# One attention block and two gated products on one core: the first pair's output product in seven products, and some steps put first in program order

## The chip, the cores and the metric

The kernel runs on one core of one Trainium2 chip. The metric is device time in microseconds, from the start to the end of one execution; lower is better. The engines are named as the profile names them: PE (TensorE's matmuls), PEld (its weight loads), DVE (VectorE), ACT (ScalarE), POOL (GpSimd) and SP (SyncE, which issues nearly all transfers). PSUM has eight banks here of 128 x 512 numbers: b0 to b3 and acc0 to acc3.

## The reference

Everything is float32. Attention is of the linear kind: 8 batches, 8 heads, 576 positions, 64 features.

```
q_s = softmax of q over the features;  k_s = softmax of k over the positions
kv  = k_s^T v          (64 x 64 for each head)
x   = q_s kv           -> 4608 rows of 512
layer one:  y = (silu(x w_gate) * (x w_val)) w_out                  (512 -> 1536 -> 512)
layer two:  out = max(max(y w1, y w2), y w3) w_out2                 (512 -> 768 -> 512)
```

## The kernel before, in words

**Tiling.** The 4608 rows are nine blocks of 512. `BLOCKS` puts them in six stages: blocks 0, 1 and 2 alone, then the pairs 3+4, 5+6 and 7+8 (stages 3, 4 and 5; the first, second and third pair). In a stage the weights' columns are taken 128 at a time, F1 = 12 such tiles in layer one and F2 = 6 in layer two; p counts them by twos. A float32 product is made of three matmuls: each operand is split into a high part (a copy rounded by ACT, "hi") and a low part (the rest, a subtraction, "lo"), and high x high, high x low and low x high are summed in PSUM.

**Seven products for eight.** In a pair, the gate, value and layer-two products of a 2 x 2 arrangement of blocks are computed in seven products by Strassen's method in Winograd's form (`wino_unit`, line 1529, and `product`, line 707): sums of row blocks (t1 to t4) times sums of weight blocks, and the results put together by copies and additions that read the PSUM banks (`wino_copy`, `wino_add`, lines 806 to 818). The weights' sums are made once: stage 3 makes their parts as it goes (`make_job`, line 1458; the instructions stand at lines 681 and 685) and stores them, stages 4 and 5 load them (`wino_load_job`).

**The output product of layer one** ("O") multiplies the hidden tiles h = silu(gate) * value by w_out. Stage 3 does it in eight products: `outs` (line 1636) runs `out_product` (line 721, the matmuls at line 736) for each of 12 hidden tiles, 4 column groups and 2 halves, 3 matmuls each; the hidden tiles are split by `hidden_job` (line 1482; instructions at 789 and 803). The stages in `OUT_WINO = (4, 5)` do it in seven: `factors` (line 1676) runs `factor_product` (line 741, the matmuls at line 748) for 6 pairs of tiles, 7 products, 2 column groups, 3 matmuls each. Its left sums of hidden tiles are made by `eager` and `second_job` (lines 1361 and 1395; the instruction is `minus`, line 757), its splits by `factor_hidden_job` (line 1342; instructions at 796 and 799), and its results are put together by `out_wino` (line 1736). The sums of w_out that it needs are made in stages 1 and 2 (`SUMS_AT`) and stored. Stage 3 in the old form ends the output with `y_wino_0`, `y_wino_1` and `y_wino_late` (lines 1915 to 1951), which make layer two's operands b11 to t4.

**What sets the order of the work.** The kernel is written out by a planner that runs when the kernel is built. `walk` (line 983) goes through the list of matmul groups in PE's order, with an estimate of the time of each. Jobs that feed a group (loads, splits, differences) stand in queues (`ahead`) and are taken some microseconds before their use. Each job books time on an engine in the plan:

```
do(e, t, dur, fn)      line 881: looks for a gap of length dur at or after t, and puts the instruction there
soon(e, t, dur, fn)    line 891: books the same gap, but puts the instruction into program order at t
best(t, cost, fn)      line 901: do, on the engine (DVE or POOL, or ACT) that would end first
```

So `do` leaves what was booked earlier in front, and `soon` passes it. The engines then run their instructions in the order written, each waiting for its own semaphores; the planned times themselves are not on the chip. `soon` reports `min(u, begin) + dur`: the end as if the step began at t, or where the operation that runs at t ends.

**What empties a bank.** `wino_unit.end` (in line 1529 on) and `consumed` (line 1503) book the copy, addition, product or maximum that reads a finished bank; a later product of the same bank waits for it.

**Attention** for the next stage runs as three chains of steps (`k_steps` and `q_steps`, lines 1092 and 1132) beside the present one: maximum, subtraction, exponential, sum, multiplication, transposition, split. `advance` (line 1032) books the steps of a chain that are due up to `LOOK` (2.0 us in stage 0, 1.4 later) ahead; `slot` (line 1020) puts a chain's matmuls (`kv_mm`, line 270; `x_mm`, lines 433 to 435) into PE's order where a bank is offered. Stage 5 has none of it.

**Memory.** Tiles are claimed by tag; a claim waits for the last reader of the tile that had the place. Tags that matter here: "or" (four places of 128 x 512, weights and sums on their way), "hh" (three places for a split hidden tile), "xr" (the rows of a pair, and later sums), "s00" to "s11" (four tiles of gate values).

## Time and profile before

| what | us |
|---|---|
| median of three runs | 1521.42 |
| lowest and highest run | 1520.96 and 1523.5 |
| the profiled execution | 1522.33 |
| its span, first to last instruction | 1520.5 |
| PE busy in the span | 1458.5 (96%) |
| DVE busy | 1097.2 (72%) |
| ACT busy | 697.2 (46%) |
| mean granted clock of PE | 0.992 |

The profile is of one execution. Rows of "busy time by stretch" give the stretch in microseconds from the span's start, its length, then for each engine its busy time and, in brackets, the number of instructions; then PE's granted clock, the DMA engines' share and GB/s. Where such a row is of one line alone, only the engines that the line uses stand there. Rows of "groups of instructions" give line, engine, operation, the tile written and the tiles read, the shapes and the count, then busy time and mean duration in ns, then the engine's idle time just before them and what ended it. Matmuls are pipelined: 390 ns is the length of one from its own start to its end, and the next begins before that.

### The profile page before, as it was taken

The page shows a single profiled execution, that of the slowest core. Times are in us where ns is not written, and L with a number is a line of the kernel's source. Part 1 is how long each engine was busy: PE and PEld are TensorE (multiplying, and loading weights), DVE is VectorE, ACT ScalarE, POOL GpSimd, SP SyncE. Part 2 cuts the span into 40 slices and gives each one's busy share as a digit, 9 for nine tenths or more (in the row PEclk, how much of TensorE's full clock was granted, in tenths as well). Part 3 has the DMA queues.
Part 4 walks back from the last instruction along what each step waited for, and adds up shares of the span by engine and source line. Part 5 has one row for each costly group of instructions (what it writes and reads, how often), then busy time and mean ns, then how long its engine had stood idle before and what let it go on. Part 6 is the DMA issues. An engine that isn't in the chain of part 4 may idle for free.

```text
span 1520.5 us, 20625 instructions
## 1 busy us (share of the span) xinstructions
PE 1458.5 (96%) x6834; PEld 1177.2 (77%) x6834; DVE 1097.2 (72%) x1879; ACT 697.2 (46%) x1196; POOL 80.4 (5%) x70
## 2 busy tenths in 40 slices
PE   2899999999999999999999989999999999999998
PEld 1666688888878888878877867888877778888887
DVE  7869996787777678676579885677887755578553
ACT  3758774554566535535443344334532332245112
POOL 1000000000000000000012040000000300000000
PEclk9899999999999999999999999999999999999999
DMA  7798878878788899988578777775776576657764
GB/s 193 201 274 298 275 235 231 257 238 256 217 283 269 289 372 307 280 268 238 180 215 259 222 221 202 209 207 160 222 207 173 177 223 195 191 160 220 208 202 148
DMA packets 318729, 349.01 MB, mean 230 GB/s; under 512 B 158368, under 2 KB 197280, under 8 KB 318624
## 3 DMA queue, kind: packets, MB, share of 16 engines
q1 hardware_dynamic: 313824, 346.52, 75.2%
q10 hardware_dynamic: 4800, 1.18, 0.4%
q8 instruction: 55, 0.90, 0.3%
q14 instruction: 50, 0.41, 0.1%
HBM read 257.16 MB, written 90.44 MB: 229 GB/s over the span
## 4 chain that ended last, share of the span: by engine, by line
PE 78%; DVE 8%; DMA 6%; ACT 5%; issue 2%; SPq 1%; ACTq 0%; DVEq 0%
PE pb L715 52%; PE pacc L736 11%; PE pacc L748 4%; PE pb L736 4%; PE pb L748 3%; DMA stage<-in_moe_w_out_dram 1%; PE pkv L270 1%; PE pacc L728 1%; ACT plain L528 1%; DMA plain<-raw_V 1%; DVE hlo L803 1%; DVE tall L818 1%; DMA v_sb<-in_v_dram 1%; DMA stage<-in_moe_w_gate_dram 1%; ACT L774 1%
## 5 line engine op out<-in xcount | busy, mean ns | idle before, releaser
L715 PE MATMUL pb<-b11h,wall 128*128 128x512 f32 x756 | 270.1, 398 | 13.1 <-ACT wall L565 6.4
L818 DVE TENSOR_TENSOR tall<-tall,pb 128x512 f32<-128x512 f32 x234 | 159.9, 684 | 158.6 <-PE pb L715 146.7
L715 PE MATMUL pb<-b21h,wall 128*128 128x512 f32 x756 | 265.1, 393 | 0.0
L715 PEld LDWEIGHTS pb<-b11h,wall 128*128 128x128 f32 x756 | 142.7, 189 | 50.6 <-ACT wall L565 8.4
L715 PEld LDWEIGHTS pb<-b21h,wall 128*128 128x128 f32 x756 | 143.1, 189 | 30.7 <-ACT tall L808 0.4
L808 ACT COPY tall<-pb 128x512 f32<-128x512 f32 x117 | 68.8, 588 | 196.8 <-PE pb L715 158.6
L715 PE MATMUL pb<-b11l,wall 128*128 128x512 f32 x378 | 148.6, 393 | 0.0
L715 PE MATMUL pb<-b21l,wall 128*128 128x512 f32 x378 | 148.0, 391 | 0.0
L568 DVE TENSOR_TENSOR wall<-plain,wall 128x512 fp32r<-128x512 f32 x126 | 86.5, 689 | 38.1 <-ACT wall L565 37.5
L565 ACT CAST wall<-plain 128x512 fp32r<-128x512 f32 x126 | 77.1, 618 | 63.8 <-DVE plain L547 22.8
L736 PE MATMUL pacc<-hhi,ow 128*128 128x512 f32 x304 | 98.9, 389 | 0.1
L715 PE MATMUL pb<-t3h,wall 128*128 128x512 f32 x252 | 88.5, 392 | 3.0 <-DVE tall L818 2.9
L789 ACT CAST hhi<-tall 128x512 fp32r<-128x512 f32 x74 | 45.5, 618 | 98.3 <-DVE tall L783 79.1
L736 PE MATMUL pacc<-ow,hhi 128*128 128x512 f32 x288 | 89.0, 390 | 0.0
L715 PE MATMUL pb<-t1h,wall 128*128 128x512 f32 x252 | 88.8, 393 | 0.0
L715 PE MATMUL pb<-b22h,wall 128*128 128x512 f32 x252 | 88.7, 392 | 0.0
L715 PE MATMUL pb<-t2h,wall 128*128 128x512 f32 x252 | 88.5, 392 | 0.0
L715 PE MATMUL pb<-t4h,wall 128*128 128x512 f32 x252 | 88.0, 390 | 0.0
L715 PEld LDWEIGHTS pb<-b11l,wall 128*128 128x128 f32 x378 | 71.4, 189 | 15.2 <-issue 1.2
L715 PEld LDWEIGHTS pb<-b21l,wall 128*128 128x128 f32 x378 | 71.5, 189 | 14.5
L783 DVE TENSOR_TENSOR tall<-s,pb 128x512 f32<-128x512 f32 x81 | 54.9, 679 | 19.4 <-PE pb L715 15.1
L803 DVE TENSOR_TENSOR hlo<-tall,hhi 128x512 fp32r<-128x512 f32 x69 | 49.5, 718 | 26.4 <-ACT hhi L789 25.8
(279 smaller groups left out, 3001.5 us busy)
## 6 DMA issues: line engine op xcount, KB each, us to landing
wall<-wino_W SPq DMA_DIRECT2D x153, 256.0 KB, 3.1
wall<-wino_G SPq DMA_DIRECT2D x102, 256.0 KB, 3.2
wall<-wino_V SPq DMA_DIRECT2D x102, 256.0 KB, 3.0
ow<-parts_O SPq DMA_DIRECT2D x33, 512.0 KB, 5.5
ow<-parts_P SPq DMA_DIRECT2D x32, 512.0 KB, 5.1
wino_W<-wall SPq DMA_DIRECT2D x63, 256.0 KB, 4.5
ow<-owino SPq DMA_DIRECT2D x48, 256.0 KB, 3.5
wino_G<-wall SPq DMA_DIRECT2D x42, 256.0 KB, 4.4
```

The lines of the kernel that those rows point to most:

```text
L270: nc.tensor.matmul(out=c["pkv"][u * D:(u + 1) * D, g, :], lhsT=lhsT, rhs=rhs, start=i == 0, stop=i == R,)
L528: nc.scalar.activation(out=plain[conv[i]], in_=high.bitcast(F32), func=AF.Abs, scale=2.0 ** -112)
L565: nc.scalar.copy(out=wall[:, i:i + 2, 0], in_=plain[kind, f].rearrange("p (a n) -> p a n", a=2))
L568: eng.tensor_tensor(out=wall[:, i:i + 2, 1], in0=plain[kind, f].rearrange("p (a n) -> p a n", a=2), in1=wall[:, i:i + 2, 0], op=ALU.subtract,)
L715: nc.tensor.matmul(out=banks[bank], lhsT=a, rhs=b, start=start and n == 0, stop=stop and n == 5, skip_group_check=True,)
L736: nc.tensor.matmul(out=banks[bank], lhsT=lhsT, rhs=rhs, start=first and n == 0, stop=last and n == 2)
L748: nc.tensor.matmul(out=banks[bank[e]], lhsT=w[:, a, es], rhs=h[b], start=first and n == 0, stop=last and n == 2, skip_group_check=True,)
L783: eng.tensor_tensor(out=hidden_tile(kind, f, half, tmp), in0=s, in1=a(), op=ALU.mult if kind == "V" else ALU.max)
L789: nc.scalar.copy(out=hid[key][0], in_=st["h", key[1], key[2], key[3]])
L803: eng.tensor_tensor(out=lo, in0=st.pop(("h", key[1], key[2], key[3])), in1=hi, op=ALU.subtract)
L808: nc.scalar.copy(out=tall[:, i], in_=banks[bank])
L818: eng.tensor_tensor(out=out_, in0=tall[:, x], in1=banks[bank] if isinstance(bank, str) else tall[:, bank], op=ALU.add)
```

## The change

The list of stages that do layer one's output product in seven products, `OUT_WINO`, gets stage 3. There the tiles for the differences of p = 2 to 5 are claimed under s00 to s11 once the last value product has read them (`have["s read"]`), not under "or", which stage 3 needs for weights; two splits late in the product go to "hh" instead of "or"; the order of the differences is 5, 4, 2, 3; and the new rows' tile is claimed only when the plan's last reader of the old one has ended (`have["x end"]`). Splits of hidden tiles are kept in the order of their claims (`have["hid order"]`). Operations that empty a PSUM bank on DVE (`consumed`, `wino_unit.end`) are booked by `soon` instead of `do`, and so are the steps of attention's chains in stages 0 to 4 (`HURRY`), on DVE and ACT. Steps that go by `best` are not touched. Products 6 and 5 of a unit are kept in the plan behind two additions (`T["c22"]`, `T["c12"]`).

```diff
@@ -842,7 +842,7 @@
     ENG = {"D": nc.vector, "G": nc.gpsimd, "A": None}
     DVE_LATE = 1.0
     HASTE = 5.0
-    EASY = ()
+    HURRY = (0, 1, 2, 3, 4)
     SWITCH = 8.0
     X_WAIT = 0.0
     OWN = 1.0
@@ -1065,9 +1065,9 @@
                 ch["t"] = best(ch["t"], {"D": dur, "G": 2.0 * dur}, fn)
             elif e in ("D+", "D="):
                 t, ch["i"] = take(ch["t"])
-                ch["t"] = do("D", t, dur, fn, ch["i"])
+                ch["t"] = (soon if len(marks) - 1 in HURRY else do)("D", t, dur, fn, ch["i"])
             else:
-                ch["t"] = do(e[0], ch["t"], dur, fn)
+                ch["t"] = (soon if len(marks) - 1 in HURRY else do)(e[0], ch["t"], dur, fn)
             if e in ("D-", "D="):
                 drop(ch["i"], ch["t"])
             if DEBUG:
@@ -1343,7 +1343,7 @@
         if key not in ready or not (home or left("hh")):
             return False
         t, a, then = ready[key]
-        t = max(t, use - 9.0)
+        t = max(t, use - 9.0, 0.0 if home else have.get("hid order", 0.0))
         if home == ("or", "or"):
             if not left("or", 2):
                 return False
@@ -1353,6 +1353,8 @@
         if not home:
             t, have["hh", key] = acquire("hh", t)
         t = do("A", t, 0.62, factor_hi, key, a, home)
+        if not home:
+            have["hid order"] = t - 0.62 - LAT + 0.01
         there["hid", key] = t = do("D", t, 0.69, factor_lo, key, a)
         if then:
             then(t)
@@ -1393,7 +1395,8 @@
             have.pop(("t1 of", p))()
 
     def second_job(use, s, p):
-        if ("B", p, 0, 1) not in have or not (p < 2 or left("or")):
+        tight = s == 3
+        if ("B", p, 0, 1) not in have or not (p < 2 or tight or left("or")):
             return False
         if ("t1 of", p) in have:
             have.pop(("t1 of", p))()
@@ -1401,6 +1404,10 @@
         t = max(ready[s, "O", p, 1][0], use - 9.0)
         if p < 2:
             a2, then = lambda: xr_slot(6 + p), None
+        elif tight:
+            t = max(t, have["s read"])
+            at(t - 0.01, spare_slot, p, ("s00", "s01", "s10", "s11")[p - 2])
+            a2, then = lambda: more[p], None
         else:
             t, o = acquire("or", t)
             at(t - 0.01, spare_slot, p)
@@ -1419,19 +1426,14 @@
 
     more = {}
 
-    def spare_slot(p):
-        more[p] = sb.tile([128, TB], F32, tag="or", name="t2f", bufs=4)
+    def spare_slot(p, tag="or"):
+        more[p] = sb.tile([128, TB], F32, tag=tag, name="t2f", bufs=4 if tag == "or" else 1)
 
...
@@ -1482,12 +1484,14 @@
     def hidden_job(use, key):
         if key not in ready or not left("hh"):
             return False
-        t, h = acquire("hh", max(ready[key], use - 9.0))
-        if use - t < HASTE and key[1:] not in EASY:
+        t, h = acquire("hh", max(ready[key], use - 9.0, have.get("hid order", 0.0)))
+        if use - t < HASTE:
+            have["hid order"] = t + 0.01
             t = soon("A", t, 0.62, hidden_hi, key)
             there["hid", key] = t = soon("D", t, 0.69, hidden_lo, key, nc.vector)
         else:
             t = do("A", t, 0.62, hidden_hi, key)
+            have["hid order"] = t - 0.62 - LAT + 0.01
             there["hid", key] = t = best(t, COST, hidden_lo, key, by=use - 1.5)
         if ("tmp", key) in have:
             drop(have.pop(("tmp", key)), t)
@@ -1517,7 +1521,8 @@
         if kind == "V" and not psum:
             t = best(t, COST, consume, kind, p, i, half, a, tmp)
         else:
-            t = do("D", t, 0.69, consume, kind, p, i, half, a, tmp, nc.vector)
+            t = soon("D", t, 0.69, consume, kind, p, i, half, a, tmp, nc.vector)
+        have["s read"] = max(have.get("s read", 0.0), t)
         if wide:
             eager(s, p, i, half, t)
         elif kind != "W2":
@@ -1539,11 +1544,11 @@
                 t, T["i", k] = take(t)
                 T[k] = bank_free[bank] = best(t, COST, wino_copy, k, bank, T["i", k], engines="AD")
             elif k == 2:
-                T[1] = bank_free[bank] = do("D", max(t, T[1]), 0.69, wino_add, kind, ("t", T["i", 1]), T["i", 1], bank, nc.vector)
+                T[1] = bank_free[bank] = soon("D", max(t, T[1]), 0.69, wino_add, kind, ("t", T["i", 1]), T["i", 1], bank, nc.vector)
             elif k == 3:
-                T[0] = bank_free[bank] = do("D", max(t, T[0]), 0.69, wino_add, kind, ("t", T["i", 0]), T["i", 0], bank, nc.vector)
+                T[0] = bank_free[bank] = soon("D", max(t, T[0]), 0.69, wino_add, kind, ("t", T["i", 0]), T["i", 0], bank, nc.vector)
                 o = ("s", 1, 1) if kind == "W1" else ("t", T["i", 1])
-                u = best(max(T[0], T[1]), COST, wino_add, kind, o, T["i", 0], T["i", 1])
+                u = T["c22"] = best(max(T[0], T[1]), COST, wino_add, kind, o, T["i", 0], T["i", 1])
                 if kind == "W1":
                     have["s", 1, 1] = u
                 else:
@@ -1554,10 +1559,14 @@
             else:
                 C, i = ((0, 1), None) if k == 5 else ((1, 0), T["i", 0])
                 t = max(t, T[0])
+                if k == 6:
+                    t = max(t, T["c22"], T["c12"])
                 if kind != "W1" and k == 5:
                     t, i = take(t)
                 o = ("s",) + C if kind == "W1" else ("t", i)
-                u = bank_free[bank] = do("D", t, 0.69, wino_add, kind, o, T["i", 0], bank, nc.vector)
+                u = bank_free[bank] = soon("D", t, 0.69, wino_add, kind, o, T["i", 0], bank, nc.vector)
+                if k == 5:
+                    T["c12"] = t + 0.05
                 if kind == "W1":
                     have[("s",) + C] = u
                 else:
@@ -1814,7 +1823,7 @@
             gates["rows",] = t
             at(t, new_rows)
 
-        HOMES = ("or", "or"), ("or", "or"), ("s00", "s01"), ("s10", "s11")
+        HOMES = (("or", "or") if s > 3 else None,) * 2 + (("s00", "s01"), ("s10", "s11"))
 
         def run(p, k, done=None, slots=True, home=None):
             bank = {0: A, 4: A, 2: C, 6: C}.get(k, X)
@@ -1826,7 +1835,9 @@
         run(n, 2, after_m2, False)
         for p in range(n + 1):
             run(p, 4, after_m4)
-            if p in (1, 2):
+            if s == 3 and p < 4:
+                ahead("second", 2.0, second_job, s, (5, 4, 2, 3)[p])
+            elif s > 3 and p in (1, 2):
                 ahead("second", 2.0, second_job, s, n - 2 + p)
         for p in range(n + 1):
             if p == 1:
@@ -1843,7 +1854,7 @@
         for p in range(n + 1):
             if p == 1:
                 mark(split_b22)
-            if 0 < p < n:
+            if 0 < p < n and HOMES[p - 1]:
                 ahead("hid2", 2.0, factor_hidden_job, (s, "O", p + 1, 6), HOMES[p - 1])
             run(p, 5, after_m5)
         for p in range(2, n + 1):
@@ -1954,7 +1965,9 @@
         for c in range(2):
             if d is None:
                 dh, half = int(op[1]) - 1, int(op[2]) - 1
-                split(op, c, t0, lambda dh=dh, half=half, c=c: plain_rows(dh, half, c))
+                have["x end"] = max(
+                    have.get("x end", 0.0), split(op, c, t0, lambda dh=dh, half=half, c=c: plain_rows(dh, half, c))
+                )
                 continue
             t = t0
             if isinstance(d[1], str):
@@ -1962,7 +1975,7 @@
                 b = lambda j=have[d[1], c][1]: tall[:, j]
             else:
                 b = lambda c=c: plain_rows(*d[1], c)
-            differ(op, c, t, lambda c=c: plain_rows(*d[0], c), b)
+            have["x end"] = max(have.get("x end", 0.0), *differ(op, c, t, lambda c=c: plain_rows(*d[0], c), b))
 
     def x_plain(j, dh):
         for c in range(2):
@@ -1972,7 +1985,7 @@
 
     BLOCKS = [[0], [1], [2]] + [[j, j + 1] for j in range(3, NB, 2)]
     NS = len(BLOCKS)
-    OUT_WINO = (4, 5)
+    OUT_WINO = (3, 4, 5)
     WHOLE = {(0, "O", f, 0) for f in range(2, F1)}
     SUMS_AT = [(1, "W1", 0), (1, "W2", 0), (1, "W3", 0), (2, "V", 5), (2, "W3", 0), (2, "W2", 1)]
     flow = []
@@ -2125,7 +2138,7 @@
         mark(lambda: alone.__setitem__(0, False))
         wide = s in OUT_WINO
         if wide:
-            mark(lambda: at(clock[0], new_rows))
+            mark(lambda: at(max(clock[0], have["x end"]), new_rows))
         for p in range(F1 // 2):
             if p == 2:
                 mark(lambda: begin_x(s + 1))
@@ -2134,7 +2147,7 @@
                 if p and wide:
                     if p < F1 // 2 - 1:
                         factors(s, p - 1, 2 * n, (("acc0", "acc1"), ("acc2", "acc3"))[n])
-                    if n and p < F1 // 2 - 1:
+                    if n and p < (F1 // 2 - 1 if s > 3 else 3):
                         ahead("second", 6.0, second_job, s, p - 1)
                 elif p:
                     outs(s, "O", [2 * p - 2 + n], 0, F1, "parts")
```

## Rows read from the trace of the kernel before

**Rows 1.** Busy time by stretch: us, then PE PEld DVE ACT POOL, clock, DMA.

```profile
584.20:912.80 328.60, 318.07 (x1523) 257.61 (x1523) 243.58 (x424) 145.88 (x282) 45.01 (x29) 0.99 0.78 240
912.80:1226.20 313.40, 304.64 (x1395) 248.11 (x1395) 228.89 (x356) 125.10 (x202) 19.61 (x12) 0.99 0.69 197
```

**Rows 2.** Busy time by stretch: the first pair's parts, the second's middle.

```profile
584.20:729.60 145.40, 144.01 (x733) 118.26 (x733) 101.35 (x193) 71.36 (x134) 9.40 (x7) 1.00 0.85 262
729.60:773.70 44.10, 43.37 (x221) 34.62 (x221) 21.81 (x38) 20.50 (x38) 2.07 (x2) 1.00 0.68 213
773.70:885.70 112.00, 107.60 (x476) 87.15 (x475) 96.01 (x168) 42.19 (x89) 18.14 (x12) 0.98 0.72 217
885.70:912.80 27.10, 23.09 (x97) 17.58 (x96) 24.41 (x27) 11.83 (x22) 15.39 (x10) 1.00 0.84 258
1045.20:1091.50 46.30, 46.30 (x205) 38.21 (x204) 38.23 (x56) 26.87 (x43) 0.00 (x0) 1.00 0.68 213
```

**Rows 3.** The chain that ended last: start us, us, what.

```profile
1397.79 38.08 PE pb L715 x168
```

**Rows 4.** Matmuls alone by stretch: lines 736, 736, 748, 748, 270.

```profile
584.20:729.60 145.40, 26.16 (x109) 20.46 (x109) 1.00 0.85 262
729.60:773.70 44.10, 42.08 (x180) 33.22 (x180) 1.00 0.68 213
...
912.80:1045.20 132.40, 12.18 (x49) 9.20 (x49) 0.99 0.73 198
1045.20:1091.50 46.30, 46.30 (x204) 38.03 (x203) 1.00 0.68 213
...
729.60:773.70 44.10, 1.39 (x40) 1.25 (x40) 1.00 0.68 213
```

**Rows 5.** Timeline of TensorE, start of layer two: start us, us.

```profile
782.21 0.80 PE L715 MATMUL pb<-t2l,wall 128*128 128x512 f32 x1 [2.28 <-DVE t2l L455]
784.08 0.63 PE L715 MATMUL pb<-t2h,wall 128*128 128x512 f32 x1
784.51 0.63 PE L715 MATMUL pb<-b22h,wall 128*128 128x512 f32 x1
```

**Rows 6.** Groups of instructions, VectorE, the first pair's layer one.

```profile
L685 DVE TENSOR_TENSOR wall<-twos,wall 128x256 fp32r<-128x256 f32 x46 | 19.5, 427 | 9.9 <-ACT wall L681 8.6 <-DMA q_sb<-in_q_dram 1.2
L803 DVE TENSOR_TENSOR hlo<-tall,hhi 128x512 fp32r<-128x512 f32 x9 | 6.2, 688 | 4.3 <-ACT hhi L789 4.2
```

**Rows 7.** Groups of instructions, VectorE, the second pair's layer one.

```profile
L799 DVE TENSOR_TENSOR hlo<-tall,hhi 128x512 fp32r<-128x512 f32 x11 | 7.4, 683 | 3.3 <-ACT hhi L796 3.3
L757 DVE TENSOR_TENSOR tall<-h,tall 128x512 f32<-128x512 f32 x5 | 3.5, 692 | 0.2
```

**Rows 8.** Groups of instructions, VectorE, the first pair's middle.

```profile
L685 DVE TENSOR_TENSOR wall<-twos,wall 128x256 fp32r<-128x256 f32 x4 | 1.7, 417 | 0.0
```

**Rows 9.** TensorE's waits, first pair's end: us in total, times, longest.

```profile
PE pb L736 <- DVE hlo L803: 3.1, 3, 1.6
```

**Rows 10.** TensorE's waits over the whole program.

```profile
PE pb L715 <- ACT wall L565: 6.4, 4, 2.7
PE pb L715 <- DVE tall L818: 2.9, 3, 1.2
PE px L433 <- DVE tall L818: 1.7, 2, 0.9
```

**Rows 11.** Timeline in the second pair's layer two.

```profile
1124.55 1.73 DVE L225 COPY qx<-qs 32x32 f32<-32x32 f32 x4
1126.81 0.63 DVE L818 TENSOR_TENSOR tall<-tall,pb 128x512 f32<-128x512 f32 x1
1126.97 1.92 POOL L256 TENSOR_TENSOR k_sb<-k_sb,qs 128x1024 f32<-128x1024 f32 x1 [1.29 <-DMA wall<-wino_W]
1127.47 1.96 DVE L783 TENSOR_TENSOR tall<-s,tall 128x512 f32<-128x512 f32 x1
```

**Rows 12.** Instructions of line 433: ns min/median/max, first and last start.

```profile
L433 PE MATMUL px<-qt,kvhi x30: 276/310/389, 202.1 to 1178.4; 128*128 128x256 f32 x16, 128*128 128x448 f32 x4, 128*128 128x384 f32 x4, 128*128 128x320 f32 x4
```

More of the change, by code (lines that the diff above doesn't have):

```diff
@@ L1429, in fourth_job @@
         return True
-    more = {}
-    def spare_slot(p):
-        more[p] = sb.tile([128, TB], F32, tag="or", name="t2f", bufs=4)
     def whole_job(use, kind, f, key, i, home):
```

## The prediction

> **What bounds the kernel now.** I read the busy time of each engine by stretches first. In the three stages that take two blocks of rows at once (I call them pairs), PE is busy for 318.07 of 328.60 us in the first and 304.64 of 313.40 us in the second [rows 1]: the bound is the number of matmuls, and only some 9 to 10 us a pair are idle. Cut finer, the first pair has layer one (584.2 to 729.6, with the first nine outputs' products in it), the middle (the rest of the output product), layer two, and the end of the second output [rows 2]. The second pair has the same four parts, in the form that the first is to get. The reader is to see two things: PE idles little in layer one and the middle, and DVE has 101.35 us of work in 145.40 us of layer one but 96.01 in 112.00 of layer two. PE is the bound, DVE is next.
>
> **The products.** In the chain of work a stretch of 168 matmuls takes 38.08 us, 0.2267 us each [rows 3], and the 204 of the second pair's middle take 46.30, the same [rows 4]. The records count 109 + 180 matmuls of line 736 in the first pair, 49 + 204 of line 748 in the second; one at a boundary is counted twice by a stretch, so 288 against 252, as 12 x 2 x 4 x 3 and 6 x 7 x 2 x 3 give [rows 4]. The change removes 36 x 0.2267 = **8.16 us** from an engine that has nothing else to do then. Layer one loses 60 of them (13.6 us, to 131.8), the middle gains 24 (5.4, to 46.3 + 1.4 for the attention's key product that lies in it [rows 4] = 47.7).
>
> **The turn from the output to layer two.** In the old form a matmul waits 2.28 us for the split operand t2l, and the steps behind it are 0.43 us apart instead of 0.2267 (784.08 to 784.51), which is the lower clock level, 1.2 GHz, after that idle time; seven such steps follow [rows 5]. Together 2.28 + 7 x 0.20 = 3.7 us. The second pair, in the new form, has no idle in the middle (46.30 of 46.30) [rows 2], and its next unit takes b22 late, as the new order does. I take **-3.7 us**; bounds 0 (the same wait under another name) and -4.4 (all idle of that part).
>
> **DVE in the first pair.** The new form swaps ten splits of layer one (line 803, 6.2 us for nine, 6.9 with the tenth) for eleven (line 799, 7.4), and adds fourteen differences by line 757, of which the row of five is 3.5 us: 14 x 0.69 = 9.7 [rows 6, 7]. The first pair alone also makes its weights' parts (line 685, 46 in layer one, 19.5 us) [rows 6], which the second pair does not. So layer one goes to 101.35 - 6.9 + 7.4 + 9.7 = 111.5 of 131.8 us, 85% against 70%. The middle goes to the second pair's 38.23 plus what only the first has there: four of line 685 (1.7) [rows 8], and eight kinds of attention step, none over 1.2 us, 4.6 by the same view: 44.5 of 47.7, 93% against 49%. Layer two keeps its work. ACT stays far off: 71.36 of 145.40 and 26.87 of 46.30 [rows 2].
>
> What does a DVE that full cost PE? Nearest row for 85%: layer two of the first pair, 86% busy, idles 4.40 - 2.28 = 2.1 us of 112, 1.9% [rows 2, 5]. For 93%: the end of the second output, DVE 24.41 of 27.10 (90%), idles 4.0 us, 15%, 3.1 of it on low parts of hidden tiles, which are what the middle's products need too [rows 2, 9]. Layer one at 1.9% is 2.5, against 1.4 now: **+1.1** (bounds -1.4; at 15%, +18.4). The middle lies between none (the second pair's, 83%) and 15% = 7.1; I take half, 3.5, against 0.7 now: **+2.8** (bounds -0.7 and +6.4), half because 93% is past the fuller row but the tiles are asked for up to 9 us ahead.
>
> **Bank-emptying operations first.** `soon` puts them where they are ready and not where the plan had a gap. PE's waits on line 818 are 2.9 us over the program [rows 10]. Ahead of the one that ends at 1127.49 the record has the attention's copies (line 225, 1.73 us for four), not splits [rows 11], and the change moves the attention's steps forward too, so most of such waits stay. I take **-1.0**; bounds -2.9 and +2.9, as what is passed over (splits, weights' low parts) may be late in turn.
>
> **Attention's steps first.** Stages without pairs have PE free of waits except where weights are converted (6.4 us on line 565) [rows 10]. ACT and DVE there are shared between conversions and attention; **0**, bounds -6.4 and +6.4 (those waits gone or doubled). Of the attention's own products, two waited 1.7 us on line 818 [rows 10]; that can go (-1.7) or grow (below). DMA, SP and POOL: the middle's DMA share is 0.68 in either form [rows 2], so the swap of 512 KB loads for 256 KB ones costs nothing; if it did, the middle's products would wait for ow. The rest of the edit (an order among hidden splits, the rows' tile claimed only when the last reader is planned, spare tiles in s00 to s11) adds waits in claims; what queues behind them on DVE and ACT is the next split, and a PE idle in layer one or the middle pays for it. I count that in the terms above.
>
> **Sum.** -8.16 - 3.7 + 1.1 + 2.8 - 1.0 = -9.0. The profiled execution took 1522.33 us (span 1520.5 and 1.83 around it), so 1513.4; the median of the three runs is 1521.42, 0.9 lower, so **1512.5 us**. A second way: the first pair takes 328.6 us and the second, in the new form, 313.4 [rows 1]. The first also has two more of the attention's key products, so the form alone can give no more than those 15.2: 1506.2 is its floor.
>
> **Rivals.** No change is what a measurement of this kernel can't tell from 0.2%, 3 us, either way.
> (1) *More.* DVE's new load hides as in the second pair, and waits on banks go: without +1.1 and +2.8, with -1.4 and -0.7, -2.9 for -1.0, -1.7 on the attention's products: 1521.4 - 8.16 - 3.7 - 2.1 - 2.9 - 1.7 = 1502.8; half of it, 1507. For it: 46.30 of 46.30 [rows 2]. Against: the second pair makes no weights.
> (2) *DVE takes it back.* Layer one and the middle idle at 15%: +18.4 + 6.4 for the 3.9 taken: 1512.5 + 20.9 = 1533; with half of that, 1523, no change. For it: the three parts at 85 to 93%, and work sent to POOL helps little: a DVE difference beside POOL's line 256 took 1.96 us [rows 11], against a mean of 688 ns for line 803's, which read SBUF twice as it does [rows 6]. Against: layer two lives with 86%. The Trainium skill, "GPSIMD Engine Reference", Specifications, says that POOL shares its memory interfaces with DVE and that they contend when a DVE instruction has two inputs in SBUF; the trace agrees with the 1.96. It speaks against this change, which adds just such work.
> (3) *Attention's products are issued too early: slower.* `soon` books the time of the gap but reports the end as if the step began at once, so a chain's planned time runs ahead of its real one; each step is put into DVE's order while its input is still on ACT, and the bank-emptying operations behind it stand still; PE then waits at the attention's product. Price: 1.7 / 2 = 0.85 us a wait [rows 10]. The records begin 60 groups of such products, 30 in either chain's name, of which one row stands [rows 12]. With 8 more waits (6.8 us) the gain is under 3 us, from 15 more (12.8) the kernel is slower by over 3; with 20, 1529.5. For it: nothing bounds how many `soon`s stand at one time. Against: two such waits now, and the chain looks only 1.4 to 2 us ahead. The Trainium skill, "TensorE: Matmul & The Clock Gate", its table of specifications, calls ScalarE's and VectorE's queues strict FIFO; line 818 behind the copies of line 225 [rows 11] agrees with it.
> (4) *The form isn't reached.* Were the first pair left in eight products, only the order would change: 1520 to 1523. The list of stages says otherwise.
>
> **Chances.** Forecast, 1507 to 1518: 0.64. More, (1): 0.14. (2) 0.12, of it 0.06 no change and 0.05 slower. (3) 0.09, of it 0.03 no change and 0.05 slower. (4) 0.01. Faster 0.80 (with the remnants of (2) and (3) that still gain), same 0.10, slower 0.10. The range reaches into (1) and to the edge of no change: **1504 to 1520**.
>
> **What would show it.** Line 748 at 504 + 252 matmuls and line 736 at 288 fewer; the stretch from the first pair's start to the second's 316 to 322 us instead of 328.6; no wait on t2l; DVE over 80% in its layer one and over 90% in its middle, with 2 to 7 us idle of PE on lines 799 or 757 there. Wrong, if the middle idles over 7 us (2), if px waits more than ten times (3), or if the stages before 584 us move by over 3 us, which I put at nothing.

## The result, and the profile after

The changed kernel takes **1544.47 us** (median of four runs, 1541.34 to 1545.4) against 1521.28 for the kernel before, run beside it: the ratio is 1.0146 [1.0128, 1.0163], so it is slower, by 22 us of 1521.3. Forecast were 1512.5 us, in a range of 1504 to 1520. The profiled execution took 1545.4 us, its span 1543.6.

The page of the kernel after, busy time by engine (the whole span):

```profile
PE 1457.0 (94%) x6798; PEld 1174.1 (76%) x6798; DVE 1127.3 (73%) x1890; ACT 696.5 (45%) x1197; POOL 135.6 (9%) x100
```

Before, the same line had 6834 matmuls and POOL at 80.4 us: the 36 products are gone, TensorE is busy for 1.5 us less only, its mean granted clock being 0.987 for 0.992, and POOL has 55 us more. Busy time by stretch, after: the first pair's layer one, middle, layer two and second output (as [rows 2]), then the second pair (as the second of [rows 1]), then all that lies ahead of stage 1.

```profile
core 0: us, PE busy (x) PEld busy (x) DVE busy (x) ACT busy (x) POOL busy (x), PEclk, DMA share, GB/s
603.20:734.80 131.60, 130.09 (x673) 106.97 (x673) 107.29 (x196) 64.36 (x126) 20.81 (x13) 1.00 0.85 260
734.80:785.10 50.30, 49.03 (x246) 39.19 (x246) 44.08 (x71) 31.95 (x55) 2.92 (x2) 1.00 0.71 209
785.10:903.10 118.00, 108.39 (x475) 87.93 (x474) 94.44 (x162) 40.78 (x83) 23.29 (x14) 0.97 0.68 211
903.10:932.10 29.00, 23.36 (x97) 17.55 (x96) 24.38 (x25) 12.43 (x23) 16.30 (x11) 1.00 0.80 252
932.10:1247.60 315.50, 303.68 (x1396) 247.04 (x1396) 229.66 (x345) 125.69 (x202) 42.59 (x26) 1.00 0.68 195
0.00:251.60 251.60, 202.99 (x889) 148.11 (x890) 193.89 (x343) 153.86 (x265) 8.16 (x23) 0.95 0.77 226
```

The part that was to get shorter did: layer one and the middle take 181.9 us against 145.4 + 44.1 before. But layer two idles for 9.6 us (118.00 less 108.39) against 4.4, the second output for 5.6 against 4.0, and the stretch ahead of stage 1, to which the prediction gave nothing, is 251.6 us long where it was 235.3. TensorE's waits over the program, after (waited for: us in total, times, longest):

```profile
...
PE pb L715 <- DVE wall L568: 13.3, 6, 4.3
...
PE pb L715 <- ACT wall L565: 6.7, 6, 2.7
PE pb L736 <- DVE hlo L803: 5.4, 4, 2.0
PE px L433 <- DVE tall L818: 5.1, 3, 3.3
PE pb L715 <- DVE tall L818: 4.4, 4, 2.2
...
```

The two rows left out at the head, 15.0 and 12.0 us, belong to the kernel's start and were 14.5 and 12.2 us before. Line 568, the low part of a converted weight, is new among the longest: five of its six waits, 13.1 us, lie between 45 and 251 us. It stood at 0.8 us, one wait, in that stretch before. px on line 818 has 5.1 for 1.7, and banks on line 818 4.4 for 2.9 [rows 10].

### The profile page after: what moved, and what is told of

It is laid out like the page before. It is cut to its first block, busy times and chain, and to the rows that moved or that the text cites. A ratio compares the mean times of both kernels' runs of the same rounds, so it can differ in the third digit from the quotient of the medians.

```text
span 1543.6 us, 20742 instructions
## 1 busy us (share of the span) xinstructions
PE 1457.0 (94%) x6798; PEld 1174.1 (76%) x6798; DVE 1127.3 (73%) x1890; ACT 696.5 (45%) x1197; POOL 135.6 (9%) x100
## 4 chain that ended last, share of the span: by engine, by line
PE 77%; DVE 12%; DMA 5%; ACT 3%; issue 2%; SPq 1%; POOL 0%; DVEq 0%; ACTq 0%
PE pb L715 52%; PE pacc L736 9%; PE pacc L748 5%; PE pb L748 4%; PE pb L736 2%; DVE tall L818 2%; DMA ow<-parts_P 1%; PE pacc L728 1%; PE pkv L270 1%; DVE hlo L803 1%; DMA stage<-in_moe_w_out_dram 1%; DMA plain<-raw_V 1%; DVE tall L783 1%; DVE h L783 1%; PE px L433 1%
## 5 line engine op out<-in xcount | busy, mean ns | idle before, releaser
L715 PE MATMUL pb<-b11h,wall 128*128 128x512 f32 x756 | 271.6, 401 | 22.9 <-DVE wall L568 13.3
L748 PE MATMUL pacc<-hhi,ow 128*128 128x512 f32 x248 | 82.2, 390 | 0.9 <-ACT hhi L796 0.9
L195 POOL PARTITION_ALL_REDUCE kb<-km x14 | 19.6, 1399 | 628.6 <-DVE km L191 601.8
L789 ACT CAST hhi<-tall 128x512 fp32r<-128x512 f32 x62 | 38.3, 619 | 73.7 <-DVE tall L783 63.5
```

Source lines behind the costliest of these rows:

```text
L195: nc.gpsimd.partition_all_reduce(c["kb"].rearrange("p h d -> p (h d)"), c["km"].rearrange("p h d -> p (h d)"), 128, bass_isa.ReduceOp.max,)
L715: nc.tensor.matmul(out=banks[bank], lhsT=a, rhs=b, start=start and n == 0, stop=stop and n == 5, skip_group_check=True,)
L748: nc.tensor.matmul(out=banks[bank[e]], lhsT=w[:, a, es], rhs=h[b], start=first and n == 0, stop=last and n == 2, skip_group_check=True,)
L789: nc.scalar.copy(out=hid[key][0], in_=st["h", key[1], key[2], key[3]])
```

## The experiments

For each kernel I took the time of the first matmul of line 715 in each stage, and in each pair that of the first in layer two, and compared the lengths of the parts with those in the trace of the kernel before. In us, longer is positive; "rest" is what lies ahead of stage 0, stages 1, 2 and 5. The last column is their sum, up to the last such matmul. A row is of one execution, which can lie off the median: e9's took 5.7 us more than its median, e12's 3.7 more, e5's and e7's 3.0 less.

| kernel | stage 0 | first pair, layer one + middle | layer two + end | second pair, layer one + middle | layer two + end | rest | sum |
|---|---|---|---|---|---|---|---|
| after | +16.1 | -7.7 | +8.0 | -3.7 | +5.7 | +5.4 | +23.8 |
| e4 seven alone | -1.0 | -8.4 | -2.6 | -1.6 | -0.9 | +0.5 | -14.0 |
| e1 no hurry | +5.3 | -8.4 | +3.2 | -2.4 | -2.7 | +4.1 | -0.9 |
| e7 before, drains | +6.0 | -1.7 | +1.5 | -2.5 | -3.2 | +2.1 | +2.2 |
| e5 before, hurry | +8.9 | +2.8 | +12.1 | +2.6 | +5.0 | +7.7 | +39.1 |
| e2 hurry from 1 | +7.7 | -5.7 | +7.1 | -1.2 | +5.2 | +3.8 | +16.9 |
| e8 landing late | +10.4 | -7.3 | +7.7 | -3.2 | +5.2 | +1.0 | +13.8 |
| e12 drains in pairs | +0.4 | -8.7 | +3.0 | -3.7 | -3.3 | +5.6 | -6.7 |
| e9 no POOL | +17.7 | -6.6 | -7.7 | +3.8 | -6.6 | +1.8 | +2.4 |
| e10 seven, no POOL | -1.9 | -7.5 | -3.1 | -2.6 | -7.9 | +1.4 | -21.6 |
| e11 no hurry, no POOL | +6.1 | -3.5 | +1.1 | +0.6 | -1.8 | +8.2 | +10.7 |
| e14 before, no POOL | -2.2 | -0.4 | -2.9 | +2.8 | -7.9 | +0.3 | -10.3 |
| e15 seven, hurry 3 | -0.3 | -0.9 | +2.2 | -3.2 | -7.9 | +1.0 | -9.1 |
| e16 end booked | +7.0 | -10.2 | +1.6 | -3.2 | -1.7 | +7.2 | +0.7 |
| e17 end booked, no POOL | +6.0 | -8.9 | -3.8 | -3.4 | -7.7 | +10.3 | -7.5 |
| e18 no hurry, booked | +7.4 | -6.5 | -4.2 | -3.6 | -8.6 | +5.8 | -9.7 |
| e19 seven, booked | +6.0 | -5.0 | -1.3 | -3.4 | -7.9 | +4.8 | -6.8 |
| e20 pairs booked | -1.8 | -8.7 | -4.9 | -3.2 | -8.6 | +2.7 | -24.5 |
| e21 and hurry 3, 4 | -1.1 | -9.1 | -3.6 | -3.1 | -7.7 | +1.7 | -22.9 |

### Each part alone: seven products, bank-emptying first, attention first

**e1**: the change without attention's steps first.

```diff
-    HURRY = (0, 1, 2, 3, 4)
+    HURRY = ()
```

> The changed kernel with attention's steps booked as before in every stage (the list of hurried stages empty); seven products and bank-emptying operations first stay. Theory H (attention's steps put first stand in VectorE's order before their loads have landed and hold up the weight conversions behind them, worth some 16 us in stage 0, 4 at the end of stage 2 and 6 in the second pair's layer two): stage 0 ends where it did before, within 2 us, and the time falls by 16 to 32 us, to 1512 to 1528. Theory S (seven products fill VectorE and cost more than they save): the time stays above 1535. Theory B (bank-emptying operations first is what costs): it stays above 1535 too.

1521.59 us, 1.0013 [1.0, 1.0027]: inside H's range. So attention's steps first cost some 20 us, though stage 0 does not come back to its old length; 5.3 us of it stay.

**e4**: also without the operations that empty a bank; what is left is the output product in seven.

```diff
-    HURRY = (0, 1, 2, 3, 4)
+    HURRY = ()
...
-            t = soon("D", t, 0.69, consume, kind, p, i, half, a, tmp, nc.vector)
+            t = do("D", t, 0.69, consume, kind, p, i, half, a, tmp, nc.vector)
...
-                u = bank_free[bank] = soon("D", t, 0.69, wino_add, ...)
+                u = bank_free[bank] = do("D", t, 0.69, wino_add, ...)
```

> Of the change the seven products alone: attention's steps and bank-emptying operations booked as before. Theory H: the prediction's own terms without the last two, -8.2 for the matmuls, -3.7 for the turn, +3.9 for VectorE's load, so 1510 to 1517. Theory S: 1525 or more, with TensorE idle over 10 us in the first pair's layer one and middle. Theory B: as H, and at least 10 us below the kernel that keeps bank-emptying operations first.

1508.02 us, 0.9915 [0.9891, 0.9939], below the expected range. By the ratios on 1521.3 us, the seven products give -12.9 us, the bank-emptying operations first then +14.9, and attention's steps first +20.2. Busy time by stretch in this kernel, columns as above, the first pair's four parts:

```profile
583.80:715.30 131.50, 130.28 (x673) 106.83 (x672) 108.64 (x208) 64.32 (x126) 5.74 (x4) 1.00 0.87 268
715.30:764.90 49.60, 49.07 (x247) 39.29 (x246) 43.19 (x71) 32.03 (x55) 1.36 (x1) 1.00 0.67 200
764.90:876.00 111.10, 107.19 (x481) 87.00 (x480) 96.10 (x170) 41.61 (x85) 12.85 (x8) 1.00 0.73 227
876.00:901.30 25.30, 21.93 (x91) 16.47 (x91) 22.59 (x23) 12.43 (x23) 14.44 (x9) 1.00 0.87 271
```

VectorE is busy for 108.64 of 131.50 and 43.19 of 49.60 us here, and TensorE idles for 1.2 and 0.5.

**e7** and **e5** put the two orders into the kernel before: e7 the bank-emptying operations (the four `do` of e4's diff to `soon`), e5 attention's steps in stages 0 to 4 (the two lines in `advance`).

> The kernel before with one edit: the operations that empty a bank in the pairs put first. Theory H: 1518 to 1525, as this touches only the pairs and the waits it can remove are under 3 us. Theory B: slower by 8 us or more, 1529 or above. Theory S: within 3 us of 1521.

> The kernel before with one edit: attention's steps of stages 0 to 4 put first. Theory H: slower by 16 to 26 us, 1537 to 1547, and 14 to 20 us of it by the end of stage 0. Theories S and B: within 3 us of 1521.

e7 takes 1527.3 us, 1.0041 [1.0026, 1.0056]: slower than H's range allowed, faster than B's. The expectation took this edit to touch the pairs alone; `consumed` runs in stages 0 to 2 as well, and 6.0 us of the loss lie in stage 0. e5 takes 1563.7, 1.0285 [1.0258, 1.0313], more than any of the theories expected. Some tiles of e5 hold other values than meant, probably because the order among hidden splits that the change keeps by hand is not kept there (not tested); it has 20626 instructions for 20625, and its time is read as that of the same work. Either order costs without the seven products, too: the loss is not only an interaction with them.

### Stage 0

Where does stage 0 lose 16.1 us? VectorE's timeline in the kernel after, then TensorE's behind it (start us, us, what, and in brackets the idle time before it and what ended it):

```profile
99.64 0.68 DVE L568 TENSOR_TENSOR wall<-plain,wall 128x512 fp32r<-128x512 f32 x1
103.97 1.22 DVE L230 TENSOR_REDUCE qm<-q_sb 128x32 f32<-128x1024 f32 x1 [3.65 <-DMA q_sb<-in_q_dram]
```

```profile
114.34 1.22 PE L715 MATMUL pb<-b11h,wall 128*128 128x512 f32 x2 [4.23 <-DVE wall L568]
115.36 0.63 PE L715 MATMUL pb<-b11l,wall 128*128 128x512 f32 x1
115.79 0.63 PE L715 MATMUL pb<-b11h,wall 128*128 128x512 f32 x1
116.22 0.63 PE L715 MATMUL pb<-b21h,wall 128*128 128x512 f32 x1
```

VectorE stands still for 3.65 us at q's maximum, whose load has not landed, while the conversions of weights wait behind it in its order. Ten microseconds later TensorE waits 4.23 us for one of them, and its next matmuls start 0.43 us apart (granted clock 0.50 from 114.34 to 118.78, the 1.2 GHz level), where 0.23 is the rule. Two more waits on line 568, of 4.3 and 2.8 us, end at 131 and 148. In the kernel before that maximum ran at 106.4 with no idle time ahead of it. The Trainium skill, "TensorE: Matmul & The Clock Gate", its table of specifications, calls VectorE's queue strict FIFO; the 3.65 us agree.

Ahead of the wait that ends at 131, VectorE is not idle at all. From 119.69 until the conversion starts at 130.49, 7.8 of its 10.8 us are steps of attention that stand in front of it, of which these are the longest:

```profile
119.69 1.22 DVE L237 TENSOR_TENSOR q_sb<-q_sb,qm 128x1024 f32<-128x1024 f32 x1
120.82 1.22 DVE L237 TENSOR_TENSOR qown<-qown,qm 128x1024 f32<-128x1024 f32 x1
...
122.89 1.20 DVE L247 TENSOR_REDUCE qs<-q_sb 128x32 f32<-128x1024 f32 x1
...
126.72 1.16 DVE L247 TENSOR_REDUCE qs<-qown 128x32 f32<-128x1024 f32 x1
...
130.49 0.63 DVE L568 TENSOR_TENSOR wall<-plain,wall 128x512 fp32r<-128x512 f32 x1
```

**e2**: attention first in stages 1 to 4 only (`HURRY = (1, 2, 3, 4)`). **e8**: all stages, but stage 0's loads are planned to land later.

```diff
-                ch["loaded", fn[0]] = t + 4.5
+                ch["loaded", fn[0]] = t + (8.5 if len(marks) == 1 else 4.5)
```

> The changed kernel with attention's steps put first in stages 1 to 4 only, not in stage 0. Theory H0 (of what attention's steps first costs, stage 0, where weights are converted, is the greater part): the time falls from 1544.5 by 9 to 14 us, to 1530 to 1536, and stage 0's end comes back to where the kernel without hurried steps has it. Theory P (the cost lies in the pairs, where work goes over to POOL and slows VectorE): it falls by under 4 us.

> The changed kernel with one number of the plan altered: in stage 0 the planner takes a load of attention's operands to land 8.5 us after its issue and not 4.5, so the steps that wait for it are put later into VectorE's order; they still go first. Theory L (stage 0 loses because a maximum over q is put ahead of conversions before its load has landed, and VectorE stands idle): the 3.65 us of idle before line 230 goes, and stage 0 ends 5 to 11 us earlier, 1533 to 1540 in all. Rival (conversions are only pushed back by attention's own work, landed or not): within 3 us of 1544.5.

e2 takes 1537.78 us, 1.0108 [1.0089, 1.0127]: about 6 us below the change, between H0's and P's numbers; its stage 0 is at +7.7, where H0 wanted e1's +5.3. e8 takes 1536.34, 1.0101 [1.0083, 1.0118], as L had it: stage 0 gets back 5.7 of 16.1 us. The idle time ahead of that maximum, in the view of line 230 of the kernel after and then of e8:

```profile
  DMA q_sb<-in_q_dram: 3.6, 1
```

```profile
  DMA q_sb<-in_q_dram: 0.9, 1
```

So a planned landing that is too early is shown as part of the loss, 5.7 us. But it is not what TensorE waits for at line 568: with VectorE's standstill down to 0.9 us, those waits are as long as ever. The same row for stage 0 of the kernel after, of e8, of e16 (below) and of e2:

```profile
PE pb L715 <- DVE wall L568: 13.1, 5, 4.3
PE pb L715 <- DVE wall L568: 13.8, 7, 5.8
PE pb L715 <- DVE wall L568: 7.3, 4, 3.9
PE pb L715 <- DVE wall L568: 1.0, 1, 1.0
```

They go when attention's steps of stage 0 are not put first (e2), and are nearly halved by the end that `soon` reports (e16, where the standstill stays at 3.8 us). What e8 gives back lies in other waits, those on line 565 among them (2.1 us for 5.1). The 5 to 8 us that stay in e1, e2 and e7 have another place: the attention's product for stage 1. TensorE's timeline in e7:

```profile
223.64 0.39 PE L433 MATMUL px<-qt,kvhi 128*128 128x256 f32 x1 [1.08 <-ACT qt L414]
227.17 0.58 PE L434 MATMUL px<-qt,kvhi 128*128 128x256 f32 x1 [3.14 <-DVE qt L418]
```

Two of its steps stand in TensorE's order 4.2 us before their operands, the high and the low part of the transposed q, which ACT and VectorE make, and the matmuls behind them run at the lower level again (granted clock 0.50 from 227.17 to 231.40). The same two waits stand in e1 and in e2. **e12** takes attention first out and keeps `soon` for `consumed` only in pairs (`do if alone[0] else soon`).

> Seven products; operations of `consumed` that empty a bank go first in the pairs only, not in stages 0 to 2; attention's steps as before; POOL stays. Theory X (stage 0's loss of 5 us without hurried attention is one product of attention, put into TensorE's order before its operand qt, which then waits 3.3 us, because the end of the operation before it was reported too early): stage 0 ends within 1.5 us of the kernel before, 1513 to 1518 in all. Rival (stage 0 loses by the order of its conversions however the drains are booked): stage 0's end stays 4 us late, 1520 to 1523.

1511.41 us, 0.9941 [0.9924, 0.9957], a little below X's range; stage 0 is at +0.4, with no px wait there. So what remained of its loss came from the bank-emptying operations of the single stages. That the early end is why, as X says, e12 does not show: with the booked end (e18, below) attention's products still wait 5.0 us in stage 0, on other operands, and stage 0 is at +7.4.

### Layer two of the pairs: POOL

POOL's groups of instructions, after (busy us, mean ns, idle before):

```profile
L783 POOL TENSOR_TENSOR h<-s,tall 128x512 f32<-128x512 f32 x15 | 24.7, 1649 | 254.4 <-DVE tall L818 238.2 <-DMA wall<-wino_V 16.1
```

The kernel before has no such group: fifteen products of hidden tiles have gone to POOL, and more of attention's steps (thirteen on lines 237 and 256, for six before). What an operation on POOL does to VectorE stands in the timelines of the first pair's layer two, VectorE's and then POOL's, where those on POOL are attention's:

```profile
818.41 2.17 DVE L783 TENSOR_TENSOR h<-s,tall 128x512 f32<-128x512 f32 x1
...
823.64 0.68 DVE L783 TENSOR_TENSOR h<-s,tall 128x512 f32<-128x512 f32 x1
...
826.46 2.40 DVE L418 TENSOR_TENSOR qtlo<-tall,qthi 128x512 fp32r<-128x512 f32 x1
```

```profile
818.12 1.92 POOL L256 TENSOR_TENSOR k_sb<-k_sb,qs 128x1024 f32<-128x1024 f32 x1 [1.20 <-DVE qs L253]
...
826.02 2.29 POOL L237 TENSOR_TENSOR qown<-qown,qm 128x1024 f32<-128x1024 f32 x1 [4.30 <-DVE qm L234]
```

The same operation takes 0.68 us with POOL idle and 2.17 beside POOL; VectorE has then to catch up, and TensorE waits behind it, as in the second pair, where a maximum of attention's stands in front of the bank-emptying addition as well:

```profile
1140.20 1.92 POOL L256 TENSOR_TENSOR k_sb<-k_sb,qs 128x1024 f32<-128x1024 f32 x1 [8.46 <-DVE qs L253]
1140.49 2.17 DVE L783 TENSOR_TENSOR h<-s,tall 128x512 f32<-128x512 f32 x1
...
1142.59 1.20 DVE L230 TENSOR_REDUCE qm<-qown 128x32 f32<-128x1024 f32 x1
1143.72 0.67 DVE L818 TENSOR_TENSOR tall<-tall,pb 128x512 f32<-128x512 f32 x1
...
1144.45 0.50 PE L715 MATMUL pb<-t1h,wall 128*128 128x512 f32 x1 [2.16 <-DVE tall L818]
```

**e9** is the change with POOL taken out of `best`; **e10** does the same to e4, **e14** to the kernel before, **e11** to e1, and **e15** is e10 with attention first in stage 3.

```diff
-        if alone[0]:
-            engines = engines.replace("G", "")
+        engines = engines.replace("G", "")
```

> The changed kernel with POOL taken from the planner's choice: every step that went to VectorE or POOL goes to VectorE. Theory P (with the end of a step reported too early, the plan sees VectorE as full and sends 65 operations to POOL instead of 35; VectorE's own operations beside them take about 2.1 us instead of 0.69, 51 us over in sum): the two losses of some 10 and 8 us in the pairs' layers two go at least by half, 1526 to 1537. Rival F (attention's steps in front of the bank-emptying ones are what costs there, and VectorE is too full to take 65 operations more): 1544 or slower.

> The seven products alone (booked as before) with POOL taken from the planner's choice. Theory P: 29 operations come to VectorE (20 us) and 22 us of slowed operations go, so 1504 to 1509, and TensorE's waits in the first pair's layer two no longer than with POOL. Rival F: VectorE lacks the room in the first pair, 1512 or slower.

> The kernel before with POOL taken from the planner's choice. Theory P: 35 operations come to VectorE (24 us), 22 us of slowed ones go, and waits on VectorE in the pairs' layers two shrink: 1509 to 1517, 4 to 12 us faster. Rival (POOL only hurts where the new form fills VectorE): 1518 to 1526.

> Seven products and bank-emptying operations first, attention's steps as before, POOL taken from the planner's choice. Theory P (bank-emptying first costs in the pairs only through the work that it sends to POOL): the first pair gains as much as with POOL taken away and attention first (some 14 us against the kernel before), stage 0 keeps its loss of about 5 us, 1501 to 1508 in all. Rival (bank-emptying first costs by itself, by what it passes over): 1510 or slower, with no gain over the 1521.6 of the same kernel with POOL beyond 10 us.

> Seven products, no POOL, bank-emptying operations as before, attention's steps first in stage 3 alone. Theory P: once POOL is out, hurried steps cost nothing where TensorE waits for attention's products and not for loads, and the 4 us that the first pair has over in the kernel with all steps first go: 1494 to 1500. Rival F (attention first costs by itself in the pairs): 1503 to 1512.

e9: 1518.66 us, 0.9992 [0.998, 1.0005], better than P's range: the two layers two come from +8.0 and +5.7 to -7.7 and -6.6, while stage 0 keeps its 17.7. e10: 1500.47, 0.9866 [0.9848, 0.9885], below P's range, and e14: 1512.09, 0.9948 [0.9933, 0.9963], inside it: without POOL the kernel before gains 8 us, and the seven products another 12.

The other two expectations failed. e11 takes 1531.28 us, 1.0063 [1.0046, 1.0081], where P wanted 1501 to 1508, and e15 1512.87, 0.9946 [0.993, 0.9963], where P wanted 1494 to 1500. Taking POOL out is no cure once operations go first; what is late then is shown by TensorE's waits in e11 (the two of the kernel's start left out):

```profile
PE px L433 <- ACT qt L414: 10.6, 4, 6.3
PE pb L715 <- ACT wall L565: 7.7, 4, 3.4
PE px L434 <- DVE qt L418: 3.4, 2, 3.1
```

Attention's products wait for a transposed q that the plan held to be ready. That led to the end that `soon` reports.

### The reported end

**e16**: the change, but `soon` reports the end of the gap that it books. **e17** adds no POOL to that, **e18** is e11 and **e19** e10 with the same edit (in e19 it reaches only the calls of `soon` that the kernel before has, `hidden_job`'s among them).

```diff
-        return min(u, begin) + dur + LAT
+        return u + dur + LAT
```

> The changed kernel with one line altered: a step put first reports the end of the gap that the plan booked for it, not the end as if it began at once. The order rule stays. Theory E (the early end is the cause: it lets the plan run ahead of VectorE, puts attention's products into TensorE's order before their operands, and makes VectorE look full so that work goes to POOL): POOL's two-operand instructions fall from 65 to about 35, TensorE's waits at attention's products from 9.5 us to under 4, and the time comes to 1512 to 1526. Rival O (the order itself, steps in front of conversions and splits, is the cause): 1537 or slower, as nothing is moved back.

> The same line altered and POOL taken from the planner's choice. Theory E: stage 0 loses under 8 us against the kernel before (it loses 17.7 without this line), 1503 to 1512. Rival O: stage 0 still loses over 13 us, 1515 or slower.

> Seven products, bank-emptying operations first with the booked end, attention's steps as before, no POOL. Theory E: the 10.6 us that attention's products wait on qt in the same kernel with the early end fall under 3, and the time from 1531 to 1499 to 1510. Rival O: 1522 or slower.

> Seven products, nothing else of the change put first, no POOL, and the booked end for the two helpers of the kernel before that already went first (the splits of hidden tiles under five microseconds of slack, and the first output's operands). Theory E: 1496 to 1502, the same or a little faster than the 1500.5 with the early end. Rival O: the same 1500.5.

e16: 1521.92 us, 1.0008 [0.9997, 1.0019], as E had it: 21 us back by one line. Its POOL is at 75.7 us for 135.6, and no product of line 783 goes there. Stage 0 gets back 9.1 us, the two layers two 6.4 and 7.4. Two marks were missed. The waits of px are 8.1 us for 9.5, where E wanted under 4: in the pairs they fall from 8.1 us to 1.7, in stages 0 to 2 they grow from 1.4 to 6.4. And the 3.8 us of idle at q's maximum stayed, since that is the landing's. e17: 1512.78, 0.9956 [0.9941, 0.997], just past E's edge. The two cures overlap: by the ratios POOL taken out gives 23 us (e9), the booked end 21, both together 29. e18: 1511.82, 0.9947 [0.9932, 0.9962], by the ratios 18 us better than e11, 2 short of E. Among its waits:

```profile
PE px L433 <- ACT qthi L414: 3.9, 1, 3.9
PE px L434 <- DVE qtlo L418: 3.6, 3, 2.9
```

The wait on qt is gone, a smaller one on its split has come; in all, the waits of px are 13.9 us for 15.6 in e11. As in e16 they fall in the pairs, from 11.3 us to 4.7, where the table has the gain, and grow in stages 0 to 2, from 4.2 to 9.2. e19 failed: 1514.98, 0.9965 [0.9954, 0.9976], 14.5 us slower than e10, where 1496 to 1502 was expected. 8 of them lie in stage 0. Its waits show the same two tiles:

```profile
PE px L433 <- ACT qthi L414: 3.7, 1, 3.7
PE px L434 <- DVE qtlo L418: 3.4, 2, 2.9
```

So the older calls of `soon` are better off with the early end, in this schedule. A reading that fits, not tested: they are splits that TensorE waits for, few at a time, and a later end moves the attention's steps behind them.

### A version that beats both

**e20**: seven products, no POOL, and the bank-emptying operations first in pairs only, with the booked end, by a function of their own; `soon` is left as it was. **e21** adds attention's steps by `ahead_of` in stages 3 and 4.

```diff
+    def ahead_of(e, t, dur, fn, *a):
+        u, i = gap(e, t, dur)
+        busy[e].insert(i, (u, u + dur))
+        at(t, fn, *a)
+        return u + dur + LAT
...
-            t = soon("D", t, 0.69, consume, kind, p, i, half, a, tmp, nc.vector)
+            t = (do if alone[0] else ahead_of)("D", t, 0.69, consume, kind, p, i, half, a, tmp, nc.vector)
...
```

> Built from the findings: seven products, no POOL in the planner's choice, bank-emptying operations first in the pairs only and with the booked end, the older helpers and attention's steps as before. Theory E: the order rule itself is harmless in the pairs once the end is right: 1494 to 1502, no slower than the 1500.5 of the seven products without it. Rival O (the order rule costs by itself): 1506 or slower.

> The kernel of the run before with attention's steps of stages 3 and 4 first too, with the booked end. Theory E: within 5 us of that run, either way, and no wait of TensorE at attention's products over 2 us. Rival O: slower than it by 8 us or more.

e20: **1497.57 us**, 0.9851 [0.9836, 0.9866]. e21: 1498.06, 0.985 [0.9834, 0.9867]. Both as expected, but for one px wait of 2.1 us in e21. The two pairs in e20, as [rows 1]:

```profile
584.10:899.10 315.00, 306.54 (x1488) 250.42 (x1487) 263.96 (x482) 149.59 (x286) 4.58 (x4) 1.00 0.79 242
899.10:1200.70 301.60, 300.34 (x1395) 247.87 (x1394) 225.97 (x371) 122.72 (x201) 2.13 (x2) 1.00 0.71 208
```

The second pair has 1.3 us of idle TensorE left of 8.8, the first 8.5 of 10.5. In the pairs the order by itself, attention's steps included, does no harm here once POOL is out and the booked end is reported; nor does it give anything that can be told from e10 (0.9851 against 0.9866, the intervals overlap).

## Why the prediction was wrong

**The products, the turn, VectorE: right, and a little too careful.** Line 748 has 252 matmuls in the first pair, and the program 36 fewer. For layer one, middle and turn together the sum had -8.16 - 3.7 + 1.1 + 2.8 = -8.0; in e4 the first pair gives -8.4 and -2.6, that is -11.0. The products and the turn (-2.6 in layer two and end, for -3.7) are about right; the wait on t2l is gone from TensorE's waits. Mis-sized were the two terms for a full VectorE: with 83% and 87% busy (forecast 85% and 93%), layer one idles 1.2 us and the middle 0.5, as before, so +1.1 and +2.8 should have been nothing. Half of a 15% idle share taken from the end of the second output was a bad neighbour: there POOL runs for 15.39 of 27.10 us [rows 2], in the middle for 1.4, and with POOL taken out the kernel before idles about 1.3 us in that part instead of 4.0, with no wait on line 803 left there (e14).

**"Bank-emptying operations first: -1.0; bounds -2.9 and +2.9": the first step that failed.** It costs 14.9 us in the changed kernel, 6 in the kernel before. I looked only at the operations passed over in the waits on line 818. Not seen was that the reported end feeds everything that is planned after it: `best` finds VectorE booked and POOL free (e1's POOL is at 117.3 us for e4's 72.3), and in the pairs attention's products are put into TensorE's order before their operands; e18 against e11 shows it, 18 us. Nor did I see that the single stages have such operations, too: in stage 0 attention's products wait 4.2 us, with the lower clock behind it, and e12 shows that these waits come with the bank-emptying operations there. By which step they come stays open, as the booked end leaves such waits in stage 0 (e18).

**"Attention's steps first: 0; bounds -6.4 and +6.4": the second and larger.** 20.2 us. By the table (after against e1) 10.8 us of it lie in stage 0 and 13.2 in the pairs' layers two. The bounds were the waits on line 565 doubled. The wait that came in stage 0 is on line 568, the same conversion's other half on VectorE, behind attention's own steps: 13.1 us for 0.8. The load that lands late is worth 5.7 us there, but not by these waits (e8). In the layers two the loss goes with POOL (e9) and, for the most part, with the reported end (e16). A bound taken from a wait that exists says nothing about a wait that an edit can create; the row to read was VectorE's order in stage 0, with attention's steps beside the conversions.

**Rival (3) had the cause, not the place or the price.** It said that the planned time of a chain runs ahead of its real one, because `soon` reports the end as if the step began at once, and that VectorE's order then stands still; it gave 1529.5 us and a chance of 0.09. e16 shows that cause: 21 us by that line alone. But it counted waits of 0.85 us at px; px waits eight times after, 9.5 us, short of more than ten that I had set as the mark, and e16 leaves 8.1 us of them, though only 1.7 in the pairs. The greater part lies at the weights' conversions in stage 0 and in the layers two. Of the marks that I gave, two spoke: stages before 584 us, "which I put at nothing", moved by 19, and from the first pair's start to the second's it is 328.9 us, not 316 to 322.

**Rival (2) had the price of POOL right** (1.96 us there, 2.03 to 2.40 here) **and its cause wrong**: the work goes to POOL because of the reported ends, not because of the fourteen differences; e4, which has them all, uses POOL less (72.3 us) than the kernel before (80.4). The Trainium skill, "GPSIMD Engine Reference", Specifications, says that the two engines contend when VectorE reads two inputs in SBUF; 2.17 against 0.68 us for one operation agrees.

**Open.** Why the booked end costs 14.5 us in e19, why stage 0 still loses 6 to 7 us with it (e16 to e18), and why attention first in stage 3 costs 12 us in e15 where in e9, with more of it, the first pair is at -14.3. Each variant is another schedule and leaves single waits of 2 to 6 us in other places; I found no rule that predicts these.

## What to carry to other kernels

An instruction that is put first in an in-order engine's program is only as early as its latest input: price such an edit by the loads and steps of other engines that feed it, with the estimates that the old order hid, and by the work behind it that now comes later. One optimistic end in a planner moves everything planned after it, on other engines too; here it cost 21 us. That is no rule for every call, as e19 shows: change the calls one kind at a time. And work sent to a second engine can slow the first by more than it takes over: try the kernel once without it.

## What the runs showed of the hardware

A VectorE operation of 128 x 512 numbers with two inputs in SBUF took 2.0 to 2.4 us in the rows read here where it ran beside a POOL operation, and 0.68 alone. An operation on POOL can so cost VectorE more than the 0.69 us that it spares there: without POOL the unchanged kernel is 8 us faster (e14). TensorE's matmuls start 0.43 us apart for ten steps, the first somewhat longer, after a wait of 4.23 us (114.34 to 118.78, granted clock 0.50), and 0.23 apart soon after (granted clock 1.00 from 119.37): such a stall costs more than its own length. Not each one does: after the wait of 2.8 us that ends at 148.16 they start about 0.23 apart, at a granted clock of 1.00.
